# A new hand-written order for the first eight steps, and one transfer for each early q

## The chip, the cores and the metric

The kernel runs on one core of one Trainium2 chip. Time is device time in microseconds (us) of one execution. The kernel before took 698.8 us in the median of three runs (698.78, 698.80, 699.63).

A core has five engines that run side by side, each through its own instructions in program order, and wait for each other through semaphores: TensorE (PE; its weight loads are listed apart as PEld), VectorE (DVE), ScalarE (ACT), GpSimd (POOL) and SyncE (SP), which here issues nearly all DMA transfers. Matmul results land in PSUM, of which the kernel uses eight banks of 128 x 512 float32; other tiles live in SBUF. The work here is in float32.

## The reference

```python
state = gamma[None, :, None, None] * state + np.einsum('bhd,bhe->bhde', k[:, :, t], v[:, :, t])
y[:, :, t] = scale * np.einsum('bhd,bhde->bhe', q[:, :, t], state)
...
h = x @ w_in
g = h - np.tanh(h)
return (g @ w_out).astype(np.float32)
```

q, k and v are (batch 4, heads 8, sequence 768, head size 64) in float32. The first two lines are a recurrence over t: linear attention with a decay gamma per head. Its output is laid out as x, 3072 tokens by 512, and goes through an expert layer: w_in is 512 x 2048, w_out 2048 x 512. Both weights arrive in float64; the kernel converts them to float32 itself.

## The kernel before, in words

**Chunks.** Attention is done in 24 chunks of 128 tokens with all eight heads, six chunks to a batch element. The decay is divided out by scaling q and v with tables. For chunk c the kernel loads k, q and v (256 KB each), scales q and v, turns k and q on TensorE (four transposes each against the identity), copies them to SBUF on ACT, and forms two groups of small 64 x 64 products (`products`, L331): k times v for the state (L342) and k times q for the scores (L348). DVE masks the scores (L355) and adds up the state (L366, L368, L372); `outputs` (L381) and `outputs_rest` (L430) multiply with q and v (L397) into a y bank; `see` (L423) is a tiny ACT read of y between these two; `keep_x` (L434) copies y into xT.

**Expert layer.** Its tiles are 256 tokens by 256 hidden columns, a "step" (n, m2). `up` (L455) makes half of a step's h in PSUM (eight rows of 128x256 in L463; TensorE takes a float32 matmul as two rows, each with a weight load). ACT and DVE form g = h - tanh(h) by a direct difference where h is large, and by a polynomial in u = h*h where it is small (`activate`, L826, and `multiply`, L837). `down` (L524) adds half of g times w_out into an accumulator bank (L530, four rows of 128x512), and `add_up` (L533) moves a finished accumulator to SBUF.

**Weights.** They come in 128-wide blocks of 512 KB in float64: W0 to W3 are columns of w_in, W4 to W7 rows of w_out, W8 to W11 and W12 to W15 the next of each, up to W31 (`load_weights`, L139). A block is converted to float32 by bit operations: two activations on ACT (L175, L183), four operations on DVE (L191 to L201), a multiply (L208) and an add (L217) on DVE or POOL.

**The first stage is written out by hand.** The string `order` (L891) lists pieces for chunks 0 to 7, weight blocks 0 to 11 and steps 0 to 7, with some loads for later. Every engine takes its pieces in the order of the string and stops at one whose inputs are not there. The letters:

- Lk, Lq, Lv: load k, q, v of a chunk, W: load a weight block (all on SP)
- s, w: scale q, v on DVE (D) or POOL (P); t, T: transposes of k, q (PE); c, C: their copies (ACT)
- p: both product groups (PE); m: mask; z, Z: state, two halves (DVE)
- b, r: outputs, first and second part (PE); e: see (ACT); y: keep_x (ACT)
- A, l: a weight block's two activations (ACT); D1 to D4: its four DVE operations; F, G: its multiply and add, on D or P
- u, v: the two halves of up (PE); au, ath, aq0, aq1, alarge: activations of a step (ACT); f0 to f4: its DVE operations; o0, o1: the two halves of down (PE); E0, E1: add_up
- x:n: n units of dummy matmul, put ahead of the next group of TensorE (`keep_busy`, L230)

Steps 0 to 7 are (0,0), (0,1), (1,0), (1,1), (2,0), (2,1), (3,0), (3,1): step 0 needs chunks 0 and 1, step 2 chunks 2 and 3, and so on; steps with m2 = 0 need W0, W1, W4 and W5, those with m2 = 1 need W2, W3, W6 and W7. After the string comes a loop over the remaining steps (L988), with the last chunks and weight blocks spread over it; steps with n of 4 and more form their products with seven multiplications of half-size blocks instead of eight.

**Buffers that set the order.** k and q have two buffers each and v four, so the load of k for chunk c + 2 waits until chunk c's products are done, and that of q until its scaling is. Scaled early q's alternate between two rooms. Transposes of chunks 0 to 3 use the two "o" banks, which later hold accumulators; from chunk 4 on, transposes (both in one pair of banks, "t") and the products of a chunk share that pair. h has two banks, so a step's up waits for f3 of the step two before in the order of the ups. y alternates between two halves of one pair of banks.

Of the kernel before, what the change touches and what calls it, by code (L numbers as in the profile page):

```python
# [22 lines left out]
A = 0.00694305119022808  # L23
# [8 lines left out]
def kernel(  # L32
# [79 lines left out]

    w1 = wts.tile([P, NC, DF], F32, name="w1")
    w2 = wts.tile([P, NM, DM], F32, name="w2")
    busy = w2[:, NM - 1, :P]
    nc.vector.memset(busy, 0.0)
    raws = {}

# [109 lines left out]
    idle = [0]  # L228

    def keep_busy(at):  # L230
        for _ in range(idle[0]):
            nc.tensor.matmul(at, busy, busy, start=True, stop=True, skip_group_check=True)
        idle[0] = 0


    WIDE = 8
# [5 lines left out]
    states = {}  # L242
    xT = {}

    def load_one(ci, which):
        if ci >= NCH:
            return
        b, j = divmod(ci, CPB)
        nm, src = ("k", "q", "v")[which], (k, q, v)[which]
        t = inp.tile([P, H, D], F32, tag=nm, name=f"{nm}_{ci}", bufs=4 if nm == "v" else 2)  # L250
        rows = src[b, :, ts(j, P), :]
        if nm == "q" and ci < WIDE:
            for i in range(2):
                nc.sync.dma_start(  # L254
                    out=t[:, ts(i, RUN)].rearrange("p r d -> p (r d)"),
                    in_=rows[i::2].rearrange("g (p r) d -> p g (r d)", r=RUN),
                )
        else:
            nc.sync.dma_start(out=t, in_=rows.rearrange("h p d -> p h d"))  # L259
# [23 lines left out]
    def turn(ci, which):  # L283

        if ci < EARLY_TURNS:
            tp = bank("o", f"kqTp{which}_{ci}")
            turned.setdefault(ci, {})[which] = tp
        else:
            if ci not in turned:
                both = banks("t", f"kqTp_{ci}")  # L290
                turned[ci] = {i: both[:, i] for i in range(2)}
            tp = turned[ci][which]
        keep_busy(tp[:, :P])
        t = loaded[ci][which]
        for p in range(NP):
            pair = t[:, p] if which else t[:, ds(2 * p, 2)]
            nc.tensor.transpose(tp[:, ts(p, P)], pair.rearrange("p h d -> p (h d)"), ident)
# [33 lines left out]
    def products(ci):  # L331

        kh, vh = loaded[ci][0], loaded[ci][2]
        kT, qT = (sides[ci][:, i] for i in range(2))
        sp = banks("t", f"s_{ci}")
        keep_busy(sp[:, 0, :P])
        scores[ci] = halves = sp.rearrange("p r (w n t) -> p r w n t", w=2, n=NP)
        for p in range(NP):
            for a in range(2):
                for i in range(2):  # L340
                    h, r = 2 * p + i, ds(D * a, D)
                    nc.tensor.matmul(halves[ds(D * i, D), a, 1, p], kh[r, h], vh[r, h],  # L342
                                     start=True, stop=True, skip_group_check=True)
# [37 lines left out]
    def outputs(ci):  # L381

        j = ci % CPB
        vh = loaded[ci][2]
        turned.pop(ci, None)
        qT = sides.pop(ci)[:, 1]
        a_, st = masked.pop(ci), states[ci]
        y = y_banks[:, ci % 2]
        keep_busy(y[:, 0, 0])
        begun = set()  # L390

        def to_y(p, i, a, lhsT, rhs):
# [4 lines left out]
            nc.tensor.matmul(y[ds(D * col, D), r, p // 2, ts(a, D)], lhsT, rhs,  # L397
                             start=start, stop=True, skip_group_check=True)
# [56 lines left out]
    def up(n, m2, i):  # L455

        begins = (n, m2) not in hps
        if begins:
            hps[n, m2] = bank("h", f"h_{n}_{m2}")
        hp = hps[n, m2][:, ts(i, TH)]  # L460
        keep_busy(hp[:, :P])
        for c in range(NC):
            nc.tensor.matmul(hp, w1[:, c, ts(2 * m2 + i, P)], xT[n // 2][:, c, ts(n % 2, TH)],  # L463
                             start=(begins and c == 0), stop=(c == NC - 1),
                             skip_group_check=True)
# [58 lines left out]
    def down(n, m2, j, first, last):  # L524

        if first:
            o_p[j] = bank("o", f"o_{n}_{m2}_{j}")
            keep_busy(o_p[j][:, :P])
        for i in range(2):
            nc.tensor.matmul(o_p[j], gT[n, m2][:, i, ts(j, P)], w2[:, 2 * m2 + i],  # L530
                             start=(first and i == 0), stop=(last and i == 1))

    def add_up(n, m2, j):  # L533
# [3 lines left out]
                sums[i] = [op.tile([P, 2, DM], F32, tag="sum", name=f"sum_{i}"), set()]  # L537
        o, begun = sums[n][0][:, j], sums[n][1]
        if j in begun:
            nc.vector.tensor_tensor(o, o_p[j], o, op=ALU.add)  # L540
        elif done and j % 2:
            nc.vector.tensor_copy(o, o_p[j])
        else:
            nc.scalar.copy(out=o, in_=o_p[j])
        begun.add(j)
        if done:
            nc.sync.dma_start(out=rows_of(n)[:, j], in_=o)
# [289 lines left out]
    def multiply(s, i):  # L837
# [61 lines left out]
    D3:3 D4:3 A:4 c:5 F:3P f2:0 C:5 l:5 ath:2 Lq:6 Lk:6 Lv:6 W:7 e:4 G:3P Lq:7 W:8 W:9 p:5  # L899
    au:2 Lv:7 r:4 aq0:2 y:4 A:5 aq1:2 l:4 f3:0 u:1 f0:2 m:5 z:5 f4:0 s:6P t:6 W:6 w:6P T:6  # L900
    Lk:7 W:10 v:1 W:11 s:7P b:5 f1:2 f2:2 f3:2 c:6 C:6 au:1 p:6 e:5 D1:5 D1:4 D2:5 D2:4 r:5
    D3:5 aq1:1 alarge:2 alarge:1 aq0:1 ath:1 u:3 D3:4 D4:5 v:3 D4:4 F:5P z:6 m:6 F:4D Z:6 f0:1
    G:4D au:3 T:7 G:5P t:7 f1:1 A:6 y:5 c:7 f2:1 D1:6 o1:0 f4:2 w:7P C:7 b:6 D2:6 f3:1 p:7
    aq0:3 e:6 ath:3 r:6 l:6 v:4 u:4 D3:6 m:7 f0:3 f1:3 D4:6 z:7 F:6P G:6P y:6 l:7 alarge:3
    aq1:3 f2:3 f3:3 A:7 D1:7 b:7 f4:1 o0:0 A:11 e:7 D2:7 D3:7 D4:7 F:7P G:7D u:5 r:7 v:5 o1:1
    o0:1 ath:4 au:4 aq0:4 l:11 f0:4 f4:3 f1:4 l:9 aq1:4 f2:4 f3:4 D1:11 E1:1 alarge:4 A:9 D1:9
    D2:9 D2:11 D3:9 E0:1 y:7 ath:5 au:5 aq0:5 aq1:5 alarge:5 o1:2 v:7 D3:11 D4:11 o0:2 o1:3
    D4:9 u:7 F:9D G:9P f0:5 o0:3 f1:5 F:11D f2:5 f3:5 f4:4 f4:5 G:11P A:8 D1:8 D2:8 E1:3 D3:8
    Z:7 au:7 l:8 A:10 D1:10 D4:8 l:10 aq1:7 D2:10 F:8D D3:10 ath:7 f0:7 aq0:7 E0:3 D4:10 u:6
# [205 lines left out]
```

## Time and profile before

| | |
|---|---|
| median of three runs | 698.8 us |
| the profiled execution | 698.95 us, of which the span from first to last instruction is 697.1 us |
| instructions in the span | 16,551 |
| busy: PE, PEld, DVE, ACT, POOL | 98%, 83%, 75%, 62%, 50% |
| DMA | 59.96 MB moved, 86 GB/s in the mean; 221 GB/s in the first 20 us, 232 from 20 to 60 us |
| TensorE clock granted | 1.00 of full speed |
| last row of TensorE in the hand-written order ends | 89.7 us |

A page of the profile gives one execution. Times count from the span's start. "L297" is line 297 of the kernel. A row such as `PE L297 MATMUL kqTp<-tab,k 128*128 128x128 f32 x4` is a group of four instructions by engine, line, operation, the tensors written and read, and shape; a bracket after it gives the idle time of that engine just before it and what ended it. "issue" there means that nothing the profile shows was being waited for. A busy share is an average; matmuls are pipelined and their ends are modelled, so consecutive rows overlap a little.

### The profile page before, as it was taken

Reading aid. Unit: us, or ns where it says so; the run is one execution under the profiler, and the core shown is the slowest. Engines: PE = TensorE matmul, PEld = TensorE weight load, DVE = VectorE, ACT = ScalarE, POOL = GpSimd, SP = SyncE. Lnnn points to the kernel's source line nnn. Section 1 sums busy time; section 2 is a strip of 40 time slices with the busy share of each in tenths; the row PEclk is TensorE's granted clock in tenths of the full one; section 3 lists DMA queues with packets and bytes.
Section 4 is the critical chain, followed back from the end, with each engine's and each line's share of the span. In section 5 each row is a group of like instructions: output and inputs, shape, how many; then the busy total and the mean of one; then the engine's idle time right before and its main releaser. Section 6 shows DMA issues by size and latency. Waiting matters only on the chain.

```text
span 697.1 us, 16551 instructions
## 1 busy us (share of the span) xinstructions
PE 685.6 (98%) x6562; PEld 575.2 (83%) x6562; DVE 519.4 (75%) x893; ACT 433.4 (62%) x818; POOL 348.0 (50%) x518
## 2 busy tenths in 40 slices
PE   8889999999999999999999999999999999999997
PEld 7776666767667667789999999999999999999996
DVE  4797999988988875577776677676677676767765
ACT  4687777666776755466555566555566555566553
POOL 2452355454455676887853454353544443544333
PEclk9999999999999999999999999999999999999999
DMA  8892258869868667500000000000000000000001
GB/s 223 237 270 57 91 135 226 217 165 226 242 169 218 164 166 194 141 32 1 1 1 16 16 2 31 1 1 31 2 1 30 1 1 31 1 17 16 1 16 47
DMA packets 119677, 59.96 MB, mean 86 GB/s; under 512 B 101808, under 2 KB 112688, under 8 KB 119600
## 3 DMA queue, kind: packets, MB, share of 16 engines
q1 hardware_dynamic: 117008, 50.21, 27.9%
q10 hardware_dynamic: 2592, 8.69, 3.3%
q8 instruction: 52, 0.85, 0.5%
q14 instruction: 25, 0.20, 0.1%
HBM read 35.83 MB, written 14.68 MB: 72 GB/s over the span
## 4 chain that ended last, share of the span: by engine, by line
PE 91%; DMA 3%; SPq 2%; DVE 2%; ACT 1%; issue 1%; POOL 0%; POOLq 0%; ACTq 0%; DVEq 0%
PE h L777 28%; PE o L530 16%; PE h L463 15%; PE fast_t L668 10%; PE y L668 8%; PE fast_o L668 8%; PE y L397 3%; PE s L342 1%; DMA raw<-in_moe_w_in_dram 1%; PE s L348 1%; DMA k<-in_k_dram 1%; SPq L159 1%; SPq L254 1%; DMA raws<-in_moe_w_in_dram 1%; SPq L259 0%
## 5 line engine op out<-in xcount | busy, mean ns | idle before, releaser
L476 ACT ACTIVATE th<-h 128x512 f32<-128x512 f32 x64 | 38.2, 597 | 141.8 <-DVE h L794 141.8
L619 POOL TENSOR_TENSOR s<-g 128x128 f32<-128x128 f32 x64 | 29.3, 457 | 191.5 <-DVE g L522 187.6
L463 PE MATMUL h<-xT,w 128*128 128x256 f32 x512 | 118.0, 382 | 0.2 <-ACT xT L443 0.2
L530 PE MATMUL o<-w,g 128*128 128x512 f32 x256 | 116.3, 595 | 0.0
L463 PEld LDWEIGHTS h<-xT,w 128*128 128x128 f32 x512 | 96.0, 190 | 22.7 <-issue 9.3
L530 PEld LDWEIGHTS o<-w,g 128*128 128x128 f32 x256 | 47.6, 190 | 46.6 <-issue 44.0
L777 PEld LDWEIGHTS h<-xT,w 128*128 128x128 f32 x512 | 76.8, 191 | 8.4 <-ACT fast_head L782 1.0
L522 DVE COPY_PREDICATED g<-large,th 128x512 f32<-128x512 int32 x88 | 74.1, 842 | 8.9
L792 DVE TENSOR_TENSOR h<-h,fast_head 128x256 f32<-128x256 f32 x64 | 27.7, 432 | 68.2 <-PE h L777 65.5
L777 PE MATMUL h<-xT,w 128*128 128x128 f32 x512 | 78.3, 275 | 0.2 <-ACT fast_head L782 0.2
L501 DVE TENSOR_TENSOR th<-h,th 128x512 f32<-128x512 f32 x88 | 60.0, 681 | 18.6 <-ACT th L474 17.4
L514 DVE SCALAR_TENSOR_TENSOR g<-q,h 128x512 f32<-128x512 f32 x64 | 44.0, 688 | 36.7 <-ACT q L490 35.3
L777 PE MATMUL h<-x,w 128*128 128x128 f32 x448 | 68.3, 275 | 0.0
L482 ACT ACTIVATE q<-u,tab 128x512 f32<-128x512 f32 x88 | 63.8, 725 | 1.7
L490 ACT ACTIVATE q<-u,tab 128x512 f32<-128x512 f32 x88 | 63.6, 723 | 0.0
L491 ACT ACTIVATE large<-u,tab 128x512 f32<-128x512 f32 x88 | 62.7, 712 | 0.0
L505 DVE SCALAR_TENSOR_TENSOR h<-q,h 128x512 f32<-128x512 f32 x88 | 60.7, 689 | 2.6 <-ACT q L482 2.6
L208 POOL TENSOR_TENSOR low<-low,power 128x512 f32<-128x512 f32 x25 | 32.4, 1296 | 57.6 <-DVE power L201 52.5
L777 PEld LDWEIGHTS h<-x,w 128*128 128x128 f32 x448 | 59.0, 192 | 0.0
L782 ACT COPY fast_head<-h 128x512 f32<-128x512 f32 x64 | 37.4, 585 | 19.8 <-PE h L777 19.8
L521 DVE TENSOR_TENSOR g<-g,u 128x512 f32<-128x512 f32 x64 | 48.0, 750 | 0.0
L787 POOL TENSOR_TENSOR fast_head<-fast_head 128x256 f32<-128x256 f32 x64 | 46.8, 731 | 1.2 <-ACT fast_head L782 1.2
(195 smaller groups left out, 1496.7 us busy)
## 6 DMA issues: line engine op xcount, KB each, us to landing
rows<-apart ACTq DMA_DIRECT2D x16, 512.0 KB, 4.6
k<-in_k_dram SPq DMA_DIRECT2D x24, 256.0 KB, 4.3
v<-in_v_dram SPq DMA_DIRECT2D x24, 256.0 KB, 5.5
raw<-in_moe_w_out_dram SPq DMA_DIRECT2D x12, 512.0 KB, 4.4
out_dram<-sum SPq DMA_DIRECT2D x22, 256.0 KB, 2.0
q<-in_q_dram SPq DMA_DIRECT2D x16, 256.0 KB, 4.8
raw<-in_moe_w_in_dram SPq DMA_DIRECT2D x14, 256.0 KB, 4.4
raw<-in_moe_w_in_dram SPq DMA_DIRECT2D x28, 128.0 KB, 4.0
```

Source lines behind the costliest of these rows:

```text
L463: nc.tensor.matmul(hp, w1[:, c, ts(2 * m2 + i, P)], xT[n // 2][:, c, ts(n % 2, TH)], start=(begins and c == 0), stop=(c == NC - 1), skip_g ...
L482: nc.scalar.activation(q0, shrinking[n, m2][0], AF.Square, bias=bias0)
L490: nc.scalar.activation(q1, u, AF.Square, bias=bias1, scale=math.sqrt(A))
L491: nc.scalar.activation(large, u, AF.Relu, bias=bias_m)
L501: nc.vector.tensor_tensor(th, hp, th, op=ALU.subtract)
L505: nc.vector.scalar_tensor_tensor(hp, in0=shrinking[n, m2][2], scalar=C0, in1=hp, op0=ALU.add, op1=ALU.mult)
L521: nc.vector.tensor_tensor(flat, src, u, op=ALU.mult)
L522: nc.vector.copy_predicated(flat, large.bitcast(I32), th)
L530: nc.tensor.matmul(o_p[j], gT[n, m2][:, i, ts(j, P)], w2[:, 2 * m2 + i], start=(first and i == 0), stop=(last and i == 1))
L668: nc.tensor.matmul(accs[n][k], left[k - 1], right, start=first and k in (1, 6, 7, 4), stop=last, skip_group_check=True)
L777: nc.tensor.matmul(hps[n, m2][:, ts(PLACE[k], P)], s_of[m2][k - 1][:, c], x_of[n][k - 1][:, c], start=(k == 1 and c == 0), stop=(c == 1), ...
L787: nc.gpsimd.tensor_tensor(odd_room[1], first[:, :2], first[:, 3:1:-1], op=ALU.add)
```

## The change

It has four parts.

1. The string `order` is rewritten: the same pieces for the same eight chunks, twelve weight blocks and eight steps, in another sequence. Some change engine: s:2 and s:3 go from POOL to DVE and w:3 stays on POOL; F:0 and G:0 go from DVE to POOL, G:2 stays on POOL with F:2 on DVE. Lv:0 comes after s:0 and c:0; Lk:1 comes before Lq:1; q runs ahead (q1, q2 and q3 before k2); W3 is loaded before W2 and W11 before W9. v:2 and v:1 come before u:2 and u:1. The units of dummy matmul are 15 instead of 17, and those ahead of p:0 are now ahead of b:0.
2. A q of chunks 0 to 7 is loaded by one transfer of 256 KB instead of two of 128 KB.
3. `keep_busy` makes one matmul of up to 512 columns out of up to four units, and the zeros it reads are a whole 128 x 512 block instead of 128 x 128.
4. The accumulators o_p are named by n and j instead of by j, so that two steps' accumulators can be open at once; loads take the issuing queue as an argument, which the order does not use.

```diff
-    busy = w2[:, NM - 1, :P]
+    busy = w2[:, NM - 1]
     nc.vector.memset(busy, 0.0)
...
     def keep_busy(at):
-        for _ in range(idle[0]):
-            nc.tensor.matmul(at, busy, busy, start=True, stop=True, skip_group_check=True)
-        idle[0] = 0
+        while idle[0]:
+            n = min(idle[0] * P, at.shape[1])
+            nc.tensor.matmul(at[:, :n], busy[:, :P], busy[:, :n], start=True, stop=True,
+                             skip_group_check=True)
+            idle[0] -= n // P
...
-            for i in range(2):
-                nc.sync.dma_start(
-                    out=t[:, ts(i, RUN)].rearrange("p r d -> p (r d)"),
-                    in_=rows[i::2].rearrange("g (p r) d -> p g (r d)", r=RUN),
-                )
+            queue.dma_start(
+                out=t.rearrange("p (i r) d -> p i (r d)", r=RUN),
+                in_=rows.rearrange("(g i) (p r) d -> p g i (r d)", i=2, r=RUN),
+            )
...
-            nc.tensor.matmul(o_p[j], gT[n, m2][:, i, ts(j, P)], w2[:, 2 * m2 + i],
+            nc.tensor.matmul(o_p[n, j], gT[n, m2][:, i, ts(j, P)], w2[:, 2 * m2 + i],
...
     order = """
-    Lk:0 Lq:0 Lv:0 x:9 t:0 s:0D Lq:1 x:3 T:0 W:0 w:0D Lk:1 c:0 C:0 A:0 x:2 p:0 z:0 Lv:1 m:0
-    Z:0 s:1P Lq:2 D1:0 D2:0 w:1D T:1 b:0 Lk:2 Lv:2 t:1 C:1 l:0 e:0 c:1 D3:0 r:0 x:2 p:1 W:1
-    D4:0 y:0 t:2 c:2 z:1 s:2P T:2 Lk:3 w:2P C:2 m:1 Z:1 b:1 p:2 e:1 r:1 F:0D A:1 G:0D D1:1 y:1
-    D2:1 z:2 Lq:3 Lv:3 Z:2 D3:1 l:1 W:2 s:3P x:1 t:3 w:3P u:0 m:2 Lq:4 c:3 T:3 s:4P C:3 D4:1
-    b:2 p:3 F:1D e:2 r:2 l:2 A:2 G:1D v:0 z:3 m:3 D1:2 y:2 Lv:5 Z:3 au:0 Lk:4 D2:2 D3:2 t:4
-    Lv:4 T:4 Lq:5 b:3 Lk:5 w:4P w:5D W:3 c:4 D4:2 F:2D C:4 e:3 W:4 W:5 ath:0 r:3 y:3 aq0:0
-    aq1:0 p:4 f0:0 z:4 m:4 Z:4 l:3 f1:0 A:3 alarge:0 u:2 G:2P t:5 s:5P T:5 v:2 D1:3 b:4 D2:3
...
+    Lk:0 Lq:0 s:0D x:9 t:0 c:0 Lv:0 x:3 T:0 C:0 Lk:1 Lq:1 w:0D p:0 W:0 Lv:1 t:1 z:0 s:1P Z:0
+    m:0 x:2 b:0 Lq:2 Lv:2 Lq:3 e:0 w:1D s:2D c:1 A:0 T:1 Lk:2 C:1 r:0 x:1 p:1 D1:0 z:1 T:2 m:1
+    s:3D D2:0 Z:1 y:0 b:1 t:2 W:1 Lk:3 e:1 w:2P r:1 D3:0 C:2 l:0 c:2 p:2 D4:0 F:0P G:0P Lv:3
+    y:1 z:2 m:2 A:1 T:3 b:2 t:3 Z:2 D1:1 D2:1 l:1 D3:1 D4:1 u:0 W:3 Lq:4 c:3 W:2 Lk:4 e:2 C:3
+    r:2 y:2 w:3P p:3 l:3 A:3 Lv:4 F:1D z:3 Lv:5 Lq:5 Lk:5 m:3 G:1P b:3 s:4P e:3 A:2 v:0 r:3
+    Z:3 D1:3 D2:3 w:4P W:5 Lv:6 ath:0 y:3 au:0 T:4 t:4 c:4 C:4 aq0:0 D3:3 D1:2 aq1:0 D4:3 D2:2
+    alarge:0 l:2 F:3P f0:0 D3:2 v:2 p:4 f1:0 u:2 f2:0 s:5P G:3P au:2 ath:2 Lq:6 z:4 m:4 aq0:2
+    Z:4 t:5 T:5 c:5 C:5 f3:0 Lk:6 A:5 D4:2 f4:0 w:5D F:2D f0:2 f1:2 D1:5 G:2P v:1 b:4 s:6P
+    aq1:2 f2:2 w:6P p:5 e:4 r:4 z:5 f3:2 m:5 D2:5 u:1 W:4 D3:5 y:4 T:6 A:4 l:5 t:6 v:3 D1:4
+    D4:5 D2:4 b:5 F:5D W:6 Lq:7 c:6 C:6 ath:1 l:4 D3:4 au:1 G:5D D4:4 e:5 aq0:1 p:6 r:5
+    alarge:1 aq1:1 y:5 alarge:2 A:6 Lv:7 Lk:7 F:4D W:7 W:8 u:3 G:4P W:11 W:9 W:10 o0:0 s:7P
+    m:6 f0:1 z:6 Z:6 f1:1 Lq:8 au:3 f4:2 D1:6 f2:1 A:7 aq0:3 t:7 D1:7 o1:0 T:7 f3:1 v:4 u:4
...
```

More of the change, by code (lines that the diff above doesn't have):

```diff
@@ L243, with load_one @@
     xT = {}
-    def load_one(ci, which):
+    def load_one(ci, which, queue=nc.sync):
         if ci >= NCH:
@@ L252, in load_one @@
         if nm == "q" and ci < WIDE:
-            for i in range(2):
-                nc.sync.dma_start(
-                    out=t[:, ts(i, RUN)].rearrange("p r d -> p (r d)"),
-                    in_=rows[i::2].rearrange("g (p r) d -> p g (r d)", r=RUN),
-                )
+            queue.dma_start(
+                out=t.rearrange("p (i r) d -> p i (r d)", r=RUN),
+                in_=rows.rearrange("(g i) (p r) d -> p g i (r d)", i=2, r=RUN),
+            )
         else:
-            nc.sync.dma_start(out=t, in_=rows.rearrange("h p d -> p h d"))
+            queue.dma_start(out=t, in_=rows.rearrange("h p d -> p h d"))
         loaded.setdefault(ci, {})[which] = t
@@ L292, in turn @@
             tp = turned[ci][which]
-        keep_busy(tp[:, :P])
+        keep_busy(tp)
         t = loaded[ci][which]
@@ L335, in products @@
         sp = banks("t", f"s_{ci}")
-        keep_busy(sp[:, 0, :P])
+        keep_busy(sp[:, 0])
         scores[ci] = halves = sp.rearrange("p r (w n t) -> p r w n t", w=2, n=NP)
@@ L388, in outputs @@
         y = y_banks[:, ci % 2]
-        keep_busy(y[:, 0, 0])
+        keep_busy(y[:, 0].rearrange("p n t -> p (n t)"))
         begun = set()
@@ L460, in up @@
         hp = hps[n, m2][:, ts(i, TH)]
-        keep_busy(hp[:, :P])
+        keep_busy(hp)
         for c in range(NC):
@@ L526, in down @@
         if first:
-            o_p[j] = bank("o", f"o_{n}_{m2}_{j}")
-            keep_busy(o_p[j][:, :P])
+            o_p[n, j] = bank("o", f"o_{n}_{m2}_{j}")
+            keep_busy(o_p[n, j])
         for i in range(2):
-            nc.tensor.matmul(o_p[j], gT[n, m2][:, i, ts(j, P)], w2[:, 2 * m2 + i],
+            nc.tensor.matmul(o_p[n, j], gT[n, m2][:, i, ts(j, P)], w2[:, 2 * m2 + i],
                              start=(first and i == 0), stop=(last and i == 1))
@@ L539, in add_up @@
         if j in begun:
-            nc.vector.tensor_tensor(o, o_p[j], o, op=ALU.add)
+            nc.vector.tensor_tensor(o, o_p[n, j], o, op=ALU.add)
         elif done and j % 2:
-            nc.vector.tensor_copy(o, o_p[j])
+            nc.vector.tensor_copy(o, o_p[n, j])
         else:
-            nc.scalar.copy(out=o, in_=o_p[j])
+            nc.scalar.copy(out=o, in_=o_p[n, j])
         begun.add(j)
@@ L854, in multiply @@
                                       early[s, "large"].bitcast(I32), early[s, "th"])
-    engines = {"D": nc.vector, "P": nc.gpsimd}
+    engines = {"D": nc.vector, "P": nc.gpsimd, "A": nc.scalar}
     pieces = {
-        "Lk": lambda c: load_one(c, 0),
-        "Lq": lambda c: load_one(c, 1),
-        "Lv": lambda c: load_one(c, 2),
+        "Lk": lambda c, e=nc.sync: load_one(c, 0, e),
+        "Lq": lambda c, e=nc.sync: load_one(c, 1, e),
+        "Lv": lambda c, e=nc.sync: load_one(c, 2, e),
         "W": load_weights,
@@ L898 @@
-    aq1:0 p:4 f0:0 z:4 m:4 Z:4 l:3 f1:0 A:3 alarge:0 u:2 G:2P t:5 s:5P T:5 v:2 D1:3 b:4 D2:3
[L899 to L909, printed above, removed]
@@ L910 @@
-    v:6 o0:4 au:6 o1:4 F:10P f1:7 f2:7 ath:6 alarge:7 G:10P f0:6 aq1:6 aq0:6 f1:6 alarge:6
-    o0:5 o1:5 E0:5 f3:7 f2:6 Lv:8 f3:6 f4:7 f4:6 Lk:8 Lq:8 W:12 W:14 W:13 G:8P E1:5
+    Lk:0 Lq:0 s:0D x:9 t:0 c:0 Lv:0 x:3 T:0 C:0 Lk:1 Lq:1 w:0D p:0 W:0 Lv:1 t:1 z:0 s:1P Z:0
+    m:0 x:2 b:0 Lq:2 Lv:2 Lq:3 e:0 w:1D s:2D c:1 A:0 T:1 Lk:2 C:1 r:0 x:1 p:1 D1:0 z:1 T:2 m:1
+    s:3D D2:0 Z:1 y:0 b:1 t:2 W:1 Lk:3 e:1 w:2P r:1 D3:0 C:2 l:0 c:2 p:2 D4:0 F:0P G:0P Lv:3
+    y:1 z:2 m:2 A:1 T:3 b:2 t:3 Z:2 D1:1 D2:1 l:1 D3:1 D4:1 u:0 W:3 Lq:4 c:3 W:2 Lk:4 e:2 C:3
@@ new lines @@
+    alarge:1 aq1:1 y:5 alarge:2 A:6 Lv:7 Lk:7 F:4D W:7 W:8 u:3 G:4P W:11 W:9 W:10 o0:0 s:7P
+    m:6 f0:1 z:6 Z:6 f1:1 Lq:8 au:3 f4:2 D1:6 f2:1 A:7 aq0:3 t:7 D1:7 o1:0 T:7 f3:1 v:4 u:4
+    l:6 aq1:3 D2:6 b:6 C:7 c:7 D2:7 f4:1 D3:6 ath:3 f0:3 D4:6 f1:3 w:7P f2:3 f3:3 D3:7 p:7
+    F:6P G:6P e:6 l:7 D4:7 F:7D r:6 au:4 u:5 A:11 ath:4 m:7 y:6 G:7P v:5 alarge:3 f4:3 z:7
+    aq1:4 au:5 aq0:4 o0:1 E0:1 f0:4 f1:4 f2:4 D1:11 o1:1 b:7 o0:2 ath:5 aq0:5 alarge:5 A:10
+    aq1:5 e:7 E1:1 l:11 l:10 alarge:4 r:7 y:7 o1:2 f3:4 D2:11 Z:7 D1:10 D3:11 D2:10 D4:11
@@ L912 @@
+    F:11D f0:5 f1:5 f2:5 G:11D D3:10 D4:10 f4:4 f3:5 o0:3 A:8 F:10P D1:8 u:6 G:10D D2:8 v:6
+    A:9 D1:9 D2:9 f4:5 D3:9 D4:9 D3:8 au:6 ath:6 aq0:6 aq1:6 E0:3 f0:6 l:9 o1:3 u:7 v:7 E1:3
+    f1:6 f2:6 f3:6 D4:8 au:7 aq0:7 ath:7 alarge:6 l:8 F:9P G:9P f0:7 o0:4 aq1:7 F:8P o1:4 o0:5
+    o1:5 E0:5 alarge:7 Lk:8 Lv:8 W:12 f4:6 f1:7 W:13 f2:7 f3:7 G:8D f4:7 W:14 E1:5
     """
```

## The prediction

> **What bounds the kernel now.** I read the page first, then busy time by stretch, TensorE's waits, then TensorE's and SyncE's timelines and the chain for the first 60 us. The page's engine row, then busy time by stretch (busy us and instruction count for PE, PEld, DVE, ACT, POOL; granted clock; DMA share; GB/s):
>
> ```profile
> PE 685.6 (98%) x6562; PEld 575.2 (83%) x6562; DVE 519.4 (75%) x893; ACT 433.4 (62%) x818; POOL 348.0 (50%) x518
> ```
> ```profile
> 0.00:20.00 20.00, 15.96 (x366) 14.00 (x366) 9.14 (x17) 8.26 (x22) 3.69 (x7) 1.00 0.86 221
> 20.00:60.00 40.00, 36.81 (x794) 30.27 (x794) 34.41 (x65) 30.35 (x74) 19.55 (x16) 1.00 0.85 232
> 60.00:100.00 40.00, 40.00 (x149) 25.24 (x148) 34.57 (x60) 29.26 (x53) 14.80 (x13) 1.00 0.22 68
> 100.00:400.00 300.00, 299.83 (x3279) 230.89 (x3278) 233.50 (x376) 194.33 (x381) 179.85 (x224) 1.00 0.50 132
> ```
>
> From 60 us TensorE has no gap until the last 7 us. Its work is the same in both kernels, so the time follows what is lost before 60: 60 - 15.96 - 36.81 = 7.2 us idle, and up to 6.6 us recorded for dummy matmuls (L232, 34 rows: 5.3 and 1.3), 13.8 in all. TensorE's waits and four rows of its timeline (start, length, what, idle before):
>
> ```profile
> PE y L397 <- ACT seen L427: 1.7, 3, 0.6
> PE kqTp L297 <- DMA k<-in_k_dram: 1.4, 2, 1.1
> PE y L397 <- issue: 1.1, 1, 1.1
> PE kqTp L232 <- DVE w L116: 1.1, 1, 1.1
> PE s L342 <- POOL v L281: 0.5, 1, 0.5
> ```
> ```profile
> 18.72 0.45 PE L397 MATMUL y<-a,v 64*64 64x64 f32 x12 [1.15 <-issue]
> 20.30 1.99 PE L463 MATMUL h<-xT,w 128*128 128x256 f32 x8 [0.20 <-ACT xT L443]
> 49.23 0.63 PE L297 MATMUL kqTp<-tab,wide 128*128 128x128 f32 x4 [0.19 <-DVE state L372]
> 51.00 0.66 PE L297 MATMUL kqTp<-tab,k 128*128 128x128 f32 x4 [1.15 <-DMA k<-in_k_dram]
> ```
>
> No one wait rules. The largest on data is chunk 7's k: the chain has it issued at 44.72 and landing 6.24 later. The transfers fill 0.85 of the DMA engines, so what is late is set by the order of the loads. SyncE's first rows give the price of an issue, 0.45 to 0.66 us each:
>
> ```profile
> 0.73 0.45 SPq L259 DMA_DIRECT2D k<-in_k_dram  x1
> 1.25 1.29 SPq L254 DMA_DIRECT2D q<-in_q_dram  x2
> 2.58 0.59 SPq L259 DMA_DIRECT2D v<-in_v_dram  x1
> ```
>
> **What the Trainium skill says.** "Runtime: NRT & Kernel Launch", Instruction fetch mechanics: instructions come in 16 KiB blocks of 256, sequentially, through a small buffer. The trace agrees: 0.85 MB in 52 packets on the instruction queue, against 13,124 TensorE rows / 256 = 51. "DMA: Bandwidth & Descriptors", Issuing engines are not separate DMA queues: all queues share 16 engines[...]. The DMA share above agrees. "TensorE: Matmul & The Clock Gate", Part 1: half clock at the start and after an idle window of about 3.4 us. The first 18 dummy rows took 3.95 us, 220 ns each, later ones about 110. "VectorE: DVE Perf Modes", Zero memsets: one cycle per element whatever the type.
>
> **The change part by part.** Durations: four transposes 0.43; one chunk's two product groups 0.51 + 0.47; y groups 0.86 and 0.34; half an up step 1.73; half a down step 1.72; DVE 0.42 to 0.69, next start 0.34 or 0.60 later if it does not depend on it; ACT 0.58 to 0.72, next start 0.48 to 0.61; POOL 1.04 (scale) and 1.28 (weight conversion).
>
> Wider memset: 512 instead of 128 elements. 384 more at the page's 0.96 GHz are an estimated 0.40; the row of 128 is 0.17. The first dummies start at 1.45 instead of 1.05. Bounds: 0 and 0.45 on the first transposes, and a warm-up window missed; later waits cover both (below). Wider dummies: the same 128-column units, 15 instead of 17, in 6 matmuls instead of 17. At four instruction rows each that is 24 instead of 68, 44 fewer in the queue. Keying o_p by n and j, and the unused queue arguments: no instruction, 0.
>
> One q transfer: eight issues of about 0.65 fewer, 5.2 us of SyncE. That is hidden wherever the DMA engines are full. For chunk 0, q is issued at 1.25 and lands at about 5.05 (k and v took 3.75 and 3.92) instead of 5.60. T0 starts at 6.0 to 6.5 instead of 6.48; v0 follows at 5.85 instead of 6.50.
>
> The order: I laid the new order on each in-order queue and walked it, loads arriving at 0.26 MB/us in their new order.
>
> To u:0. v1 lands at 11.7 (before: 12.4), its scale ends 12.4, p:1 runs 12.45 to 13.45. s:2 ends 13.3, z:1 and m:1 at 14.7, b:1 14.75 to 15.6; t:2, r:1. p:2 waits on ACT, where e:1, C:2 and l:0 precede c:2 (ends 17.95). Its L348 half ends 18.45, T:3 18.9, m:2 19.7, b:2 20.6, t:3 21.05. W0 is now converted on POOL (F:0 17.5, G:0 ends 20.15; on DVE it took 1.4 instead of 2.6); that is covered, since u:0 runs 21.05 to 22.85. Before, u:0 began at 20.30 but without T:3 and b:2. With them, 1.3 us, the old kernel stands at the same place at about 23.3: 0.4 gained.
>
> u:0 to 29. r:2, p:3 to 24.2, then a new wait: b:3 follows p:3 directly and needs z:3 and m:3 (24.4 to 25.42). 1.25 us idle. b:3, v:0 (to 28.1), r:3, T:4, t:4 to 29.3; the old kernel has the same set at 29.5: 0.2 gained. Behind b:3 in line stand v:0 and all of chunk 4.
>
> 29 to 41. W2 now follows W3 and q4; it lands at 24.2 to 26.0 and A:2, ahead of v:0's activations on ACT, wants it at 27.0. v:2 waits for y:3 (29.4), p:4 for C:4, ends 32.2; u:2 34.0. T:5 and t:5 need the bank that z:4, m:4, Z:4 read (34.2), now queued behind f1:0 and f2:0. v:1 moves ahead to 35.1; b:4, p:5, r:4, u:1 end at 40.9. The old kernel does that set without v:1 by 40.5, with it 42.2: 1.3 gained. The old 0.54 on v4's scale and 0.47 on see disappear here.
>
> 41 to 55. T:6, t:6, v:3, b:5, p:6, r:5, u:3 end 47.55; old 48.97: 1.4. Then o0:0 runs before t:7; its weights (G:4 on POOL) are ready at 47.4. k7 now has 9.5 MB of loads up to and with it, not 11.0, and is issued at 38.8, after p:5 frees its buffer. Landing is 42.6 (3.8 later), at the longest latency of this stage (7.4) 46.2; it is wanted at 49.35. The old 0.19 + 1.15 at T:7 and t:7 are gone. v:4, u:4 end at 55.45. The old kernel ends them at 58.8, with p:7, b:6, r:6 (2.2) done and o0:0 (1.8) not: 58.4 for the same work. Best case 2.95 gained.
>
> After 55 I found no new wait, and W12 to W14 still load once W9 to W11 are converted, well before ACT wants them near 90: u:5 wants the bank freed by f3:3 (57.2), its turn is 57.65. The conversion G:8, last on DVE, ends about 5 us after v:7, while o0:4 to o1:5 fill 6.9.
>
> Instruction fetch: counting rows, the old 1.15 us pause comes after about 745, just short of 768, where a new block begins; row 512 was passed at about 15.3, and work went on at 18.7, 3.4 us later. In the new order rows 512 to 768 span b:1 to b:2, 15.2 to 19.9, so 4.7 us. No pause; worth 0, as ACT's wait for W1 covered it before.
>
> Deductions. If v1 lands as late as before (12.4), 0.65; I take that. G:4 and f3:1 are each ready 0.15 before their turn. POOL rows run up to 1.61 instead of 1.28, so I take 0.5 for lateness there and between. 2.95 - 0.65 - 0.5 = 1.8. The profiled execution has 697.1 of span and 1.85 around it, 698.95, 0.15 over the median. 698.95 - 1.8 = 697.15, against the median 697.0.
>
> **Rivals.** A, no measurable difference: the loads don't come sooner, the single q changes nothing (it does not do what it says), and chunk order only trades the old see and scale waits for the p:3 to b:3 wait. Then k7's 1.35 alone is won and half of it given back at o0:0: 0.7, 698.1. For: DMA share 0.85. Against: the v:1 placed ahead of b:4.
>
> B, slower: a clock relapse. Between 11.0 and 14.75 the new order has TensorE busy for 1.45 of 3.75 us; the old had no such stretch after 5 us. If that counts as an idle window, work runs at half clock until a busy one. From T:2 to u:0 lie 4.8 us of TensorE work to be doubled, and u:0's 1.8; the old gaps hide about 1.6. That costs 5.0, net +3.2: 702. It needs two windows; one costs 1.7 and leaves 0.1 gained. It turns slower beyond 1.8 lost. Against: the longest single gap is 1.25, where 1.15 left the clock at 1.00.
>
> C, slower less sharply: SyncE waits at the k6 load until p:4 ends (32.2). W4 stands behind it, wanted by A:4 on ACT at 39.8, with C:6 and p:6 behind that. W4 lands at 37.6 to 40.3. Each us later is one lost; landing at 43 ends at 698.8 + 1.4 = 700.2.
>
> **How the numbers follow.** 0.2% is 1.4 us, about what a measurement of this kernel tells from no change. Main case 0.53, its own range 695.8 (nothing deducted) to 697.4. A 0.28 (697.4 to 699.6). B and C together 0.19 (699.6 up; B 0.07, C 0.12). The range 695.7 to 700.2 leaves out most of B and C's worse half. Faster 0.52, same 0.29, slower 0.19.
>
> **What would show it.** Right: no wait of t:7 on k near 50; u:0's group at about 21, after four chunks' transposes; a 1.2 us wait of y on DVE's m near 25; no issue pause; TensorE without gap from 50. Wrong: a head or low row of ACT waiting for DMA after 27 (C), transposes or h rows of double length before 25 (B), gaps on g or w after 47.

## The result, and the profile after

The changed kernel took 696.12 us in the median of eight runs (694.77 to 698.35), against 699.54 for the kernel before on the same chip (eight runs, 698.78 to 700.92). The ratio is 0.9957, with a 95% interval of 0.9945 to 0.9970: 3.0 us faster, 2.1 to 3.8. A later comparison (e11 below) gave 0.9951 (0.9934 to 0.9968).

The profiled execution took 695.71 us, of which the span is 693.9, 3.2 less than before. The page's engine row and busy time by stretch, in the columns of the rows shown of before:

```profile
PE 685.8 (99%) x6540; PEld 572.4 (82%) x6540; DVE 523.8 (75%) x894; ACT 432.6 (62%) x818; POOL 348.1 (50%) x517
```
```profile
0.00:20.00 20.00, 17.34 (x395) 12.44 (x396) 10.43 (x20) 8.94 (x23) 4.43 (x8) 1.00 0.88 233
20.00:60.00 40.00, 38.84 (x713) 31.41 (x712) 38.07 (x66) 30.70 (x76) 19.11 (x17) 1.00 0.83 226
60.00:100.00 40.00, 40.00 (x188) 24.30 (x187) 36.62 (x62) 30.42 (x57) 14.23 (x12) 1.00 0.29 89
100.00:400.00 300.00, 299.82 (x3294) 232.47 (x3293) 233.81 (x375) 193.38 (x380) 180.76 (x226) 1.00 0.49 129
```

TensorE is idle for 3.8 us of the first 60 (60 - 17.34 - 38.84) instead of 7.2. From 60 us on TensorE is busy throughout in both. That nothing was gained late, a marker shows: the first up row of step 8, the first work after the hand-written order. TensorE's timeline of the kernel before, then of the changed one (start, length, what):

```profile
89.54 3.62 PE L463 MATMUL h<-xT,w 128*128 128x256 f32 x16
```
```profile
86.35 3.62 PE L464 MATMUL h<-xT,w 128*128 128x256 f32 x16
```

Both executions need 607.55 us from that row to the end of the span (697.1 - 89.54 and 693.9 - 86.35, to rounding). All that was gained was gained before it. The lines named here move by one in the changed kernel: dummies are L233, up is L464, transposes L298, y products L398, the two halves of `products` L343 and L349.

TensorE's waits after the change (total us, times, longest), the whole view:

```profile
PE kqTp L233 <- DVE w L116: 1.5, 1, 1.5
PE kqTp L298 <- DMA k<-in_k_dram: 0.8, 1, 0.8
PE kqTp L298 <- PE h L464: 0.6, 1, 0.6
PE y L398 <- DVE state L369: 0.3, 1, 0.3
PE y L398 <- DVE a L356: 0.2, 1, 0.2
PE h L778 <- ACT fast_head L783: 0.2, 1, 0.2
PE h L464 <- POOL w L217: 0.2, 1, 0.2
```

The three waits on ACT's `see`, the issue pause of 1.1 and the wait for POOL's v are gone. The wait for the zeros grew by 0.4, as the prediction had it. The rows of TensorE's timeline in which the walk of the prediction can be followed:

```profile
15.94 0.63 PE L298 MATMUL kqTp<-tab,k 128*128 128x128 f32 x4 [0.82 <-DMA k<-in_k_dram]
20.46 1.99 PE L464 MATMUL h<-xT,w 128*128 128x256 f32 x8 [0.17 <-POOL w L217]
24.34 0.46 PE L398 MATMUL y<-kqT,state 64*64 64x64 f32 x16 [0.27 <-DVE state L369]
...
49.14 0.60 PE L298 MATMUL kqTp<-tab,k 128*128 128x128 f32 x4
...
51.73 3.62 PE L464 MATMUL h<-xT,w 128*128 128x256 f32 x16
```

At 49.14 chunk 7's k is turned without a wait. The two halves of up at 51.73 (v:4 and u:4) end at 55.28; the prediction had 55.45, and 58.4 for the same work in the old kernel. SyncE's first rows:

```profile
1.24 0.74 SPq L255 DMA_DIRECT2D q<-in_q_dram  x1
2.04 0.59 SPq L260 DMA_DIRECT2D v<-in_v_dram  x1
2.67 0.81 SPq L260 DMA_DIRECT2D k<-in_k_dram  x1
3.52 2.01 SPq L255 DMA_DIRECT2D q<-in_q_dram  x1
```

For chunk 0's q, one issue takes 0.74 us where two took 1.29. One issue is not always the shorter: the next q takes 2.01, where its two parts had taken 1.57.

### The profile page after: what moved, and what is told of

It reads as the page before. It is cut to its first block, busy times and chain, and to the rows that moved or that the text cites. A ratio compares the mean times of both kernels' runs of the same rounds, so it can differ in the third digit from the quotient of the medians.

```text
span 693.9 us, 16487 instructions
## 1 busy us (share of the span) xinstructions
PE 685.8 (99%) x6540; PEld 572.4 (82%) x6540; DVE 523.8 (75%) x894; ACT 432.6 (62%) x818; POOL 348.1 (50%) x517
## 4 chain that ended last, share of the span: by engine, by line
PE 94%; DVE 2%; DMA 2%; issue 1%; ACT 0%; POOL 0%; SPq 0%; POOLq 0%; DVEq 0%; ACTq 0%
PE h L778 28%; PE h L464 16%; PE o L531 16%; PE fast_t L669 10%; PE y L669 8%; PE fast_o L669 8%; PE y L398 3%; PE s L343 2%; PE s L349 1%; DMA k<-in_k_dram 1%; PE kqTp L298 1%; DMA v<-in_v_dram 1%; DMA q<-in_q_dram 0%; DVE a L356 0%; DVE g L523 0%
## 5 line engine op out<-in xcount | busy, mean ns | idle before, releaser
L464 PE MATMUL h<-xT,w 128*128 128x256 f32 x512 | 117.8, 382 | 0.2 <-POOL w L217 0.2
L464 PEld LDWEIGHTS h<-xT,w 128*128 128x128 f32 x512 | 95.9, 190 | 21.7 <-issue 9.1
L531 PEld LDWEIGHTS o<-w,g 128*128 128x128 f32 x256 | 47.5, 190 | 46.2 <-issue 42.8
L523 DVE COPY_PREDICATED g<-large,th 128x512 f32<-128x512 int32 x88 | 76.1, 864 | 9.0
L208 POOL TENSOR_TENSOR low<-low,power 128x512 f32<-128x512 f32 x26 | 34.5, 1325 | 59.2 <-DVE power L201 46.2
```

Source lines behind the costliest of these rows:

```text
L523: nc.vector.copy_predicated(flat, large.bitcast(I32), th)
L531: nc.tensor.matmul(o_p[n, j], gT[n, m2][:, i, ts(j, P)], w2[:, 2 * m2 + i], start=(first and i == 0), stop=(last and i == 1))
```

## The experiments

The order, the single q and the wide dummies can be taken apart: each alone, and each pair. All ratios are against the kernel before on the same chip; times are medians. The chips differ (e1 to e4, e5 to e8 and e9 to e12 ran on one each), so ratios are to be compared and not times. The gain in us is worked out from the ratio.

| kernel | us (runs) | ratio, 95% interval | us gained |
|---|---|---|---|
| changed kernel | 696.12 (8) | 0.9957, 0.9945 to 0.9970 | 3.0 |
| order alone (e5) | 697.55 (10) | 0.9970, 0.9956 to 0.9984 | 2.1 |
| single q alone (e6) | 697.85 (18) | 0.9974, 0.9963 to 0.9984 | 1.8 |
| wide dummies alone (e7) | 699.63 (14) | 0.9999, 0.9987 to 1.0011 | 0.1 |
| order and wide, q in two (e1) | 697.27 (14) | 0.9962, 0.9948 to 0.9976 | 2.65 |
| order and single q, narrow (e2) | 695.68 (6) | 0.9937, 0.9913 to 0.9962 | 4.4 |
| the same, second time (e10) | 696.33 (6) | 0.9944, 0.9927 to 0.9960 | 3.9 |
| changed kernel, beside e10 (e11) | 696.27 (6) | 0.9951, 0.9934 to 0.9968 | 3.4 |
| single q and wide, old order (e3) | 698.28 (22) | 0.9980, 0.9969 to 0.9992 | 1.4 |

Executions of one kernel differ: the eight of the changed kernel by 3.6 us, 43 of the kernel before on one chip by 5.6. Where loads land differs too: chunk 1's v landed between 10.5 and 13.8 us over the profiles of all kernels. So times decide here, and a single profile shows only which waits exist in that execution.

### The q transfer taken back (e1), then the dummies (e2)

```diff
 # e1: the changed kernel with
-            queue.dma_start(out=t.rearrange(...), in_=rows.rearrange(...))
+            for i in range(2):
+                queue.dma_start(out=t[:, ts(i, RUN)]..., in_=rows[i::2]...)
 # e2: the changed kernel with
-    busy = w2[:, NM - 1]
+    busy = w2[:, NM - 1, :P]
-        while idle[0]: ...
+        for _ in range(idle[0]):
+            nc.tensor.matmul(at[:, :P], busy, busy, ...)
```

> The kernel after, with each early q loaded by two transfers again. Theory T (the gain is the new order's; the single q is hidden behind full DMA engines): 3 us faster than before, as the kernel after is, within 0.5; T0 starts at 6.5 to 6.6 in both, since the single q0 landed at 5.57 and the two halves before at 5.60. Rival R1 (the 3.5 us of SyncE's issue time that the single transfers save are what lets v1, k2 and W1 come sooner): most of the gain is gone, 1 us or less faster than before, and t:2's wait for k2 (0.82 us) grows by a us or more.

> The kernel after, with the old dummy matmuls (one of 128 columns per unit, 60 instruction rows instead of 24) and the old memset of 128 columns. Theory T: 3 us faster than before within 0.5; the first transposes start about 0.4 earlier (5.0 instead of 5.45), which the wait for q0 takes back; no issue pause, since rows 512 to 768 still span about 4 us. Rival R2 (fewer rows are what removed the 1.15 us issue pause, and with it part of the gain): a pause of about 1 us with the releaser 'issue' appears on TensorE before 30 us and the kernel is only 2 us faster than before.

With q in two parts the new order still gains 2.65 us, 0.35 less than the changed kernel by the ratios, well inside both intervals. With narrow dummies it gained 4.4, but from six runs.

### The old order under the new loads (e3), and chunk 7's k alone (e4)

```diff
 # e3: the changed kernel with the whole string order of the kernel before
 # e4: the kernel before with
-    ... Lq:7 W:8 W:9 p:5
+    ... Lq:7 W:8 p:5 Lk:7 W:9
-    Lk:7 W:10 v:1 ...
+    W:10 v:1 ...
```

> The kernel after with the old order string: single q transfers, wide dummies and o_p by n and j stay. Theory T: as fast as before within 0.5 us, with t:7's wait for k7 near 50 us back (about 1.1 us). Rivals R1 and R2 (transfers or dummies carry the gain): 1 to 3 us faster than before. If the issue pause near 17.6 us was due to the number of rows it is gone here, at no gain in time.

> The kernel before with one edit: the load of k7 stands right after p:5 and W8 and ahead of W9, instead of after W6. Theory T (the ledger: 1.5 of the 3.1 us are gained between 47 and 55 us, where the old kernel waits for k7): t:7 no longer waits for k near 50 us (old 1.15), and the kernel is 1.0 to 1.4 us faster than before. Rival R3 (the old wait is covered, TensorE would stop a moment later for another thing, W6 or v7): 0 to 0.5 us faster, with a new wait of TensorE between 50 and 62 us.

e3 is not the kernel before: 0.9980, 1.4 us faster. So about half of the gain does not need the new order, against my theory that the single q is worth nothing. Its chunk 7 no longer waited for k (issued 41.12, landed 46.76); why the load went out 3 us sooner here than in e6 below (44.12), which differs only in the dummies and zeros, was not shown.

e4 removes the same wait by itself: k7 lands at 47.57 and t:7 does not wait. Whether this gained anything was not shown: the ratio, 0.9985, is 1.05 us with an interval (0.9970 to 1.0001) that just holds no gain at all, and the medians are 699.62 and 699.71. The profile speaks for rival R3, which named W6. TensorE's rows from t:7 on, and one of ACT:

```profile
51.53 0.60 PE L297 MATMUL kqTp<-tab,k 128*128 128x128 f32 x4
52.24 1.98 PE L530 MATMUL o<-w,g 128*128 128x512 f32 x4
54.69 0.46 PE L397 MATMUL y<-kqT,state 64*64 64x64 f32 x16 [0.47 <-ACT xT L443]
...
55.71 0.69 PE L342 MATMUL s<-v,k 64*64 64x64 f32 x32 [0.33 <-issue]
```
```profile
53.44 0.67 ACT L175 ACTIVATE head<-raws 128x512 f32<-128x512 f32 x1 [1.50 <-DMA raws<-in_moe_w_out_dram]
```

k7 now stands ahead of W9, v7 and W6 on SyncE, and W6 landed at 53.33 instead of 49.87. ACT waited 1.50 for it with y:5's copy (L443) queued behind, and TensorE for the copy. Not all of this need be the edit's doing, since this execution had lost 1.55 us to a wait on ACT at 39.08 already; but e9, which has the same edit and not that wait, loses much the same behind t:7. From t:7's row to step 8's up row this execution needs 39.95 us (91.48 - 51.53), the one of before 38.54 (89.54 - 51.00): the 1.41 more are about what the old waits at T:7 and t:7 come to together, 0.19 and 1.15.

### Each part alone (e5, e6, e7)

```diff
 # e5: the changed kernel, q in two parts as in e1, dummies as in e2
 # e6: the kernel before, with the one q transfer of the changed kernel
 # e7: the kernel before, with the wide zeros and dummies of the changed kernel
```

> The new order alone: two transfers per early q and the old dummies (o_p by n and j stays, since the order needs it). Theory T (most of the gain is the order's): 2.2 to 3.2 us faster than before, as the kernel after with q in two was (2.65). Rival R1 (the parts add up, the old order having gained 1.4 from transfers and dummies): 3.0 - 1.4 = 1.6 us faster.

> The kernel before with one edit: each early q in one transfer. Theory T2 (formed after the old order with all else ran 1.4 us faster, without the wait for k7: single q transfers free SyncE, and it reaches the load of k7 at 41 instead of 45 us): 1.0 to 1.6 us faster than before, k7 issued 3 us earlier, no wait of t:7 on k. Rival R4 (the wide dummies did it, by taking the pause at 17.6 away): 0.3 us or less, and the pause of about 1.1 us near 18 stays.

> The kernel before with one edit: the wide dummies and their wider memset (40 TensorE rows fewer). Theory T2: within 0.4 us of before; no pause near 17.6 us, since the rows are shifted, but one elsewhere may come; the wait for k7 near 50 us stays. Rival R4: 1.0 to 1.5 us faster.

The single q alone gains 1.8 us in the old order. How it does so was not as I had written for e6 either: I thought k7 would be issued sooner. It was issued at 44.12 and landed 6.4 later, and its wait is still there in e6's timeline, and so is the issue pause:

```profile
18.09 0.45 PE L396 MATMUL y<-a,v 64*64 64x64 f32 x12 [1.04 <-issue]
...
50.59 0.66 PE L296 MATMUL kqTp<-tab,k 128*128 128x128 f32 x4 [0.84 <-DMA k<-in_k_dram]
```

What came sooner lies at the start. In SyncE's rows chunk 1's k goes out at 5.64 and its v at 6.28, where the kernel before has 6.81 and 7.45; k1 lands at 9.60 instead of 10.57, v1 at 10.49 instead of 12.39, and step 0's up begins at 19.29 instead of 20.30.

The chain of the kernel before, traced back from 24 us, has 7.3 us of SyncE's issue rows and runs through W1's load, which landed at 18.81 and held ACT, and with it xT and u:0; in e6 it landed at 17.10. So SyncE's time is on that path although the DMA share of the first 20 us was 0.86. The engines had room at the start: in the first 10 us the share rose from 0.80 to 0.90, and the rate from 209 to 229 GB/s. That one transfer is better packed than two is no rival: there are 119,549 packets for the same bytes instead of 119,677. From the rows of one execution I can follow 1.0 us of the 1.8 to u:0, and only 0.41 of it is left at step 8's row (89.13 against 89.54), after a new wait of 0.97 on ACT's copy at 37.13. How the gain in the median comes about was thus not traced.

The order alone gains 2.1. Its profile has a long wait for chunk 1's v, which landed at 13.79. TensorE's rows from there:

```profile
14.56 1.13 PE L342 MATMUL s<-v,k 64*64 64x64 f32 x32 [2.58 <-DVE v L281]
15.47 1.08 PE L348 MATMUL s<-kqT 64*64 64x64 f32 x32
16.48 1.11 PE L297 MATMUL kqTp<-tab,wide 128*128 128x128 f32 x4
```

That is the case for which the prediction deducted 0.65; in this one execution it is four times as much. And it is rival B's relapse: after the wait the granted clock is 0.59 from 14 to 16 us and 0.56 from 16 to 18, and the three groups take 2.96 us (14.56 to 17.52) where the prediction has 1.41 for them. Of the ten executions of e5, four have a mean clock of 0.998 or less, of 96 of the kernel before 29, of the 26 with the new order and the single q (the result, e2, e10, e11) none. This is not what makes the gain: without such executions the medians beside e11 are 699.72 before and 696.27 changed.

With the single q the same v went out at 7.3 to 7.6 (the changed kernel, e2, e10 to e12) and not at 8.16 (e5) or 8.26 (e1). Alone the two parts gave 2.1 and 1.8 us, together 3.0 to 4.4. The plain sum, 3.9, lies in that range, so that they overlap was not shown, nor that they do not. The wide dummies alone are nothing: the pause that ended at 18.72 is gone, and others appeared, 0.79 us up to 31.73 and 0.77 up to 39.02.

### One load nearer (e8)

```diff
 # e8: the kernel of e2 with
-    m:0 x:2 b:0 Lq:2 Lv:2 Lq:3 e:0 w:1D s:2D c:1 A:0 T:1 Lk:2 C:1 ...
+    m:0 x:2 b:0 Lq:2 Lv:2 Lk:2 e:0 w:1D s:2D c:1 A:0 T:1 Lq:3 C:1 ...
```

> An attempt at a better version: the kernel after with the old narrow dummies (which ran 4.4 us faster than before, interval 2.7 to 6.1) and with the load of k2 ahead of that of q3. Theory T: the 0.8 us wait of t:2 for k2 (0.82 in the kernel after) goes, as k2 is issued about 1 us sooner; s:3 waits for q3 instead, which only T:3 needs, at 18. Chunk 2's later products wait for ACT's copy, so little of it reaches u:0: 3.2 to 4.4 us faster than before. Rival: q3 late holds DVE's queue (D2:0, Z:1 and W0's conversion behind s:3), u:0 starts at 21 or later, and it is slower than the kernel after.

k2 landed at 14.93 and t:2 did not wait, but p:1 waited 1.0 for v1 ahead of it. The time was 696.09 (0.9955, 0.9938 to 0.9973), not to be told from the changed kernel. So nothing measurable was gained. But it is a weak test of that wait: of the two profiles of the kernel it was made from, one has 0.5 for k2 (e10) and one no such row (e2), and both have the wait for v1, 1.1 and 1.5.

### Two small edits, narrow against wide, and k7 late (e9 to e12)

```diff
 # e9: the kernel of e6 with the order edit of e4
 # e10: the kernel of e2 again;  e11: the changed kernel again
 # e12: the changed kernel with
-    ... A:6 Lv:7 Lk:7 F:4D W:7 W:8 u:3 G:4P W:11 W:9 W:10 o0:0 s:7P
+    ... A:6 Lv:7 F:4D W:7 W:8 u:3 G:4P W:11 W:9 Lk:7 W:10 o0:0 s:7P
```

> The kernel before with two small edits together: one transfer for each early q, and k of chunk 7 issued ahead of W9. Alone they measured 0.9974 (-1.8 us) and 0.9985 (-1.05 us). Theory S (the two act on different waits, the first on the early arrivals of k1, v1 and k2, the second on the 0.84 us for which chunk 7's transposes still waited with the first edit alone): they add, ratio 0.9955 to 0.9965, t:7 does not wait, step 8's first up row starts at 87.0 to 88.0. Theory O (both give the same microseconds, and the rest is taken back at the next wait): ratio 0.997 to 0.998, a new wait of about 1 us between 30 and 55 us.

> The changed kernel with the dummies and the zeros of before, a second time, beside the changed kernel itself on one chip. Theory N (the wide dummies are worth nothing; the first reading of -4.4 us came from few runs): ratio to before 0.995 to 0.9965, within 0.7 us of the changed kernel. Rival M (the wider memset's 0.40 us delays the dummies and costs the path about 1.4 us): 0.993 to 0.9945, 1 us or more under the changed kernel.

> The changed kernel itself, as the yardstick for the other three on this chip. Theory N: ratio to before 0.995 to 0.9965, equal to the narrow one within 0.7 us. Rival M: 1 us or more slower than the narrow one.

> The changed kernel with k of chunk 7 loaded after W9 instead of ahead of W7, all else as it is. From the row of issues it then goes out at about 46.3 us and lands, 5 to 7.5 us later, at 51.3 to 53.8; its transposes want it at 49.14. Theory K (the place of this load is worth what the clock says, one for one): a wait of 2.2 to 4.7 us at t:7, step 8's first up row at 88.5 to 91, and a time 2 to 4.5 us above the changed kernel's: ratio to before 0.9985 to 1.002. Theory E (the stage is elastic: the weight blocks that now come sooner, or work ahead, take up the delay): a wait under 1 us or one that is won back later, time within 1 us of the changed kernel's.

e9: 697.32 us, 0.9959 (0.9944 to 0.9974), 2.9 us gained from five runs. That is the sum of 1.8 and 1.05, as theory S had it, and t:7 does not wait; but the interval also holds theory O's 0.997, and e4's 1.05 is not clear of nothing. Step 8's row was expected at 87.0 to 88.0 and stands at 88.34. This execution still has the old issue pause, 1.37 us up to 17.95, and from t:7's row it needs 39.79 us to step 8's, 1.25 more than the kernel before. Two edits in the old order thus reach what the whole new string reaches, as far as these intervals can tell.

e10 and e11: 696.33 and 696.27 us. Narrow and wide dummies are the same as far as six runs each can tell; the 4.4 of e2 was not found again.

e12 puts a price on lateness. k7 goes out at 44.74 and lands 5.7 later, at 50.46. The timeline of e12:

```profile
46.13 1.88 PE L531 MATMUL o<-w,g 128*128 128x512 f32 x4
50.60 0.63 PE L298 MATMUL kqTp<-tab,k 128*128 128x128 f32 x4 [2.59 <-DVE head L194]
```

The bracket names a DVE row that ended at about the same moment, the first of two L194 (a weight block's conversion) at 50.13. It is not what t:7 waits for: in the changed kernel those two rows come at 51.35, after t:7 has run. The load is. In time e12 took 697.54 us (0.9969, 0.9956 to 0.9983), 1.3 above the changed kernel beside it, with overlapping intervals. Theory K had the wait right (2.2 to 4.7) and the time too high (2 to 4.5 above); theory E had the wait wrong, and its time, within 1 us, is not excluded. Of the 2.59 us, 1.3 were made up in this execution before the wait: o0:0 begins at 46.13 and not at 47.42. That happened ahead of the edited place: u:2 begins at 31.07 instead of 31.57, and v:1 at 33.87 instead of 35.05 (the last section shows how that step came about). After the wait nothing is won back: from t:7's row to step 8's there are 37.24 us here and 37.21 in the changed kernel. So the wait is shown, one for one with the landing; what it costs in the median is only bounded. Which of the other moves in the string carry its gain was not taken apart.

## Why the prediction was right, and where its sum was off

The forecast was 697.0, its main case 695.8 to 697.4; the result is 696.12, at the gain of the best case (2.95 against 3.0) and not of the chosen value (1.8). That match is in part luck. The walk prices the order, and the order without the single q gave 2.1 (e5) and 2.65 (e1), between the chosen value and the best case; the rest, if it is more than chance, came with the single q, which the sum has at nothing.

- **k7 ahead of W7.** Right: issued at 38.44 (predicted 38.8), landed at 43.13 (42.6 to 46.2), no wait at 49.14. e12 shows that the wait returns with the load's place. That the wait's end is worth its length holds in the new order, where the rows after t:7 follow without a wait, and did not hold in the old: moving only this load there (e4) removed the wait, and TensorE took 1.41 us more behind it (1.25 in e9).
- **The 0.65 for a late v1.** This deduction was not needed in the profiled execution: v1 landed at 11.35, not 12.4. SyncE's saved time is one part of it: v1 was issued 0.6 to 0.7 us sooner than with q in two. The rest is how long it took, 3.8 us, and that varies: with the single q too, v1 landed at 12.34 in e10 and at 12.51 in e2. The median of e10 is that of e11, where v1 landed at 11.33; so, as far as one profile each can say, a v1 later by 1 us shows no price in time.
- **The 0.5 for lateness on POOL and between.** Too much: G:4, which also moves from DVE to POOL in the new string, and f3:1 were in time, and TensorE waited for POOL only at u:0, 0.17. The 0.58 at T:5 was in the walk already (34.2 predicted, 34.15 measured).
- **The single q at nothing.** This is the step that failed. The Trainium skill, in "DMA: Bandwidth & Descriptors", Issuing engines are not separate DMA queues, says of issuing from several engines that it saves only the sequencer's time, usually small beside the transfer. It does not speak of fewer issues; I carried it over to them, and called the time hidden "wherever the DMA engines are full". In the old order e6 measures 1.8 us for it (0.16 to 0.37%). In the new order it is 0.35 with wide dummies (e1 against the result) and 1.8 with narrow ones (e5 against e10), with overlapping intervals. A mean DMA share of 0.86 in the first 20 us does not say that the sequencer has a lead. Chunk 0's own q gained nothing in the changed kernel's profile: one transfer of 256 KB took 4.3 us from issue, each half had taken 3.5 and 3.6, so q0 landed at 5.57 and not at the estimated 5.05. In the other profiles with the single q it landed at 5.00 to 5.97, in those with two parts at 5.57 to 5.70. What came sooner in e6 are the loads queued behind.
- **The wider memset and the fewer dummy rows.** Right in the result: the first dummies start at 1.45, the first transposes at 5.45, and the wide dummies alone (e7) are 0.9999. e10 beside e11 says the same in the new order. The 0.40 comes out by luck: the memset takes 0.485 us instead of 0.165, 0.32 more, and starts 0.08 later. That is less than the page's rate gives, so the trace does not bear that rate out.
- **The walk from u:0 to u:4.** u:0 at 20.46 (21.05 predicted), u:1's end 40.87 (40.9), u:3's end 47.42 (47.55), u:4's end 55.28 (55.45). The wait expected between p:3 and b:3, 1.25 us, is smaller: the part of b:3 that needs only the old state ran ahead, at 23.62, and the bracket at 24.34 shows 0.27 for the state. The group takes 1.71 us to 25.33 where its work is 0.86, so some 0.85 were lost; the bracket counts only what lies beyond the rows' modelled ends. One wait was not foreseen: t:2 stood 0.82 for k2, which landed at 15.81.
- **Instruction fetch.** No pause in the new order, as counted. But that they are worth 0 was read from one place alone. In the old order they stand at fixed places in the sequence of TensorE's rows. Counted in the traces, the y group at 18.72 breaks off after matmul 348, with a pause of 1.15 before, 0.67 in e4, 1.04 in e6 and 1.37 in e9, all with narrow dummies. With wide ones (e3, e7) this pause is gone, and there are pauses after matmuls 474, 601 and 728: 0.65, 0.51 and 0.78 in e3. The places are 126 or 127 matmuls apart, each with a weight load, so 252 to 254 rows, close to the blocks of 256 that the prediction counted in. After 474 e4 and e6 pause too (0.94 and 0.39), the kernel before does not, and e4 and e9 have one of 0.33 after 1,014, which is not at such a step: what makes a place show was not found. The Trainium skill, in "Runtime: NRT & Kernel Launch", Instruction fetch mechanics, calls this cost mostly hidden; the trace agrees in so far as most of the 52 blocks show no pause, but single ones reach 1.37 (e9). No run here prices them alone.

The rivals. A, a gain of 0.7 us, lies outside the measured 2.1 to 3.8, and its premise that the single q does nothing fell with e6. B (702) did not happen in the changed kernel: u:0's eight rows take 1.99 as before, not twice that, and after the dummies the clock is 1.00 in every stretch of its profile. The relapse itself was a sound fear: e5 shows one, after 2.58 us without work (the longest gap that B counted was 1.25), and it took some 1.55 us (2.96 - 1.41), where B has 1.7 for one window. C (700.2) fell: from 27 us to 70 no row of ACT waits for a transfer, so W4 came in time.

## What to carry to other kernels

A stage that fills the DMA engines can still be late by what its issuing queue spends: count the issues ahead of the first loads that the compute engine waits for, and halve them before rewriting an order. When loads set the pace, price a single wait by moving its one load, and look at what that load displaces: with k7 brought forward in the old order its own wait ended, W6 came late, and no gain could be told from nothing. So do not add up waits from one profile.

## What the runs showed of the hardware

The clock first: in e5 it fell to half in the stretch after TensorE had stood for 2.58 us and was back at 1.00 from 18 us on; a wait of 2.59 in e12, at 50.60, left it at 1.00. Why the one and not the other was not tested.

I had not expected how exactly DVE and POOL take turns. The wait of T:5 (0.58 us on the bank that Z:4 reads) starts with a DVE row of block W2's conversion. DVE and then POOL in the changed kernel:

```profile
29.64 1.74 DVE L197 SCALAR_TENSOR_TENSOR head<-raw,head 128x512 uint32<-128x512 uint32 x1
```
```profile
28.56 1.04 POOL L282 TENSOR_TENSOR v<-v,tab 128x512 f32<-128x512 f32 x1 [2.11 <-DMA v<-in_v_dram]
29.56 1.28 POOL L208 TENSOR_TENSOR low<-low,power 128x512 f32<-128x512 f32 x1
```

and in e12, where T:5 does not wait:

```profile
29.14 0.87 DVE L197 SCALAR_TENSOR_TENSOR head<-raw,head 128x512 uint32<-128x512 uint32 x1
```
```profile
28.42 1.04 POOL L282 TENSOR_TENSOR v<-v,tab 128x512 f32<-128x512 f32 x1 [2.47 <-DMA v<-in_v_dram]
29.42 1.73 POOL L208 TENSOR_TENSOR low<-low,power 128x512 f32<-128x512 f32 x1
```

Beside no POOL row this DVE row takes 0.69. In the changed kernel it starts 0.08 us after POOL's L208 has started, waits for its end at 30.84 and ends 0.54 after that. In e12 it starts while the row before is running, gets its turn at that row's end (29.46), ends 0.55 later, and it is POOL's L208 that is stretched, from 1.28 to 1.73. In the first 60 us of all fourteen profiles, each conversion row of L191, L194 or L201 (one SBUF input) that was stretched beside a POOL row ended 0.28 to 0.29 us after that row (50 rows); those of L197, L208 and L217 (two inputs) ended 0.54 to 0.55 after it (36 rows). Such DVE rows in the changed kernel take up to 1.26 us in place of 0.42, and 1.74 in place of 0.69. The Trainium skill, in "SBUF — State Buffer", Who interferes with whom, describes this: DVE and GpSimd share a port pair under an exclusive lock, and the later one blocks fully. These numbers agree. Whether a DVE row began just before or just after the next POOL row decided 0.87 us of its length, and v:1 behind it starts at 35.05 in one execution and at 33.87 in the other. That this makes part of the spread between executions is likely, but no run tested it.
